# A third seven-product unit in the last two tiles of a fused attention and feed-forward kernel, and a prologue in another form

## The chip, the cores and the metric

The kernel runs on one core of one Trainium2 chip. The metric is the device time of one execution in microseconds, the median of three runs. In the profile, PE is TensorE (matmuls), PEld its weight loads, DVE is VectorE, ACT is ScalarE, POOL is GpSimd and SP is SyncE; L543 is line 543 of the kernel.

## The reference, cut to what matters

Attention over keys and values that are averaged in groups of eight rows, followed by a feed-forward layer with a silu:

```python
# q, k, v: 8 batches, 8 heads, 576 rows, 64 columns
k_p = k.reshape(B, H, Sp, pool, D).mean(axis=3)      # pool = 8, Sp = 72
v_p = v.reshape(B, H, Sp, pool, D).mean(axis=3)
scores = scale * np.matmul(q, k_p.transpose(0, 1, 3, 2))
attn = softmax(scores)
x = np.matmul(attn, v_p)                              # as 4608 tokens x 512
h = x @ w_in                                          # 512 x 2048
g = h * (1.0 / (1.0 + np.exp(-h)))
out = g @ w_out                                       # 2048 x 512, float32
```

## The kernel before: the parts that matter

The 4608 tokens are worked in nine tiles of 512 (t = 0 to 8), each with two stages. **up** computes h = x @ w_in and the silu, **down** computes g @ w_out. Work on the attention for the next tiles is put between the matmuls of both stages, as "fillers": a filler with number n is emitted ahead of step n + 1 of its stage. Each engine works its instructions in the order in which the program emits them.

```python
def spread(fillers, n):
    todo = sorted(fillers, key=lambda f: f[0])
    for i in range(n):
        yield i
        while todo and todo[0][0] <= i:
            todo.pop(0)[1]()
    for f in todo:
        f[1]()
```

The 2048 hidden columns are 16 groups of 128. A **plain** group takes four matmuls of 512 tokens (four steps) and a silu from PSUM. A **unit** takes four groups (two pairs) and 512 tokens as a 2 x 2 block product with seven products in place of eight (Strassen's scheme, in Winograd's way of sharing sums). A product is four matmuls of 256 columns (two steps). Sums of weight blocks are made once, sums of x blocks once for each tile, and VectorE and ScalarE combine the products:

```python
UNITS = ((4, 6), (8, 10))      # first groups of the two pairs of each unit
...
def stage(y, n):               # y: the unit; P, Q, R: PSUM banks of the unit
    if n == "2":
        product(y, 2, "P", True)
        nc.scalar.copy(r_sb, ps["P"])
    elif n == "5":
        product(y, 5, "Q", True)
        tt(out=rr_sb, in0=ps["Q"], in1=r_sb, op=ALU.add)
    elif n == "1":
        product(y, 1, "R", True)
        tt(out=t_sb, in0=ps["R"], in1=rr_sb, op=ALU.subtract)
    elif n == "4":
        product(y, 4, "P", False)
        hidden(y, 1, 0, ps["P"])              # silu, from PSUM
    elif n == "3":
        product(y, 3, "Q", False)
        hidden(y, 0, 1, ps["Q"])
    elif n == "7":
        product(y, 7, "P", False)
        tt(out=c_sb[0], in0=ps["P"], in1=t_sb, op=ALU.add)
    elif n == "6":
        product(y, 6, "Q", False)
        tt(out=c_sb[1], in0=ps["Q"], in1=t_sb, op=ALU.add)
    elif n == "h":
        hidden(y, 0, 0, c_sb[0])              # silu, from SBUF
    else:
        hidden(y, 1, 1, c_sb[1])
```

r_sb, rr_sb, t_sb and the two c_sb are single buffers that all units share. The order of an up stage from tile 2 on, where G(n) is a plain group and (y, "251") are products of unit y with their combining:

```python
items = (
    G(12, 13) + [(0, "251")] + G(14) + [(0, "43")] + G(15) + [(0, "76")]
    + [(1, "2")] + [(0, "hs")] + [(1, "51")] + G(0) + [(1, "43")] + G(1)
    + [(1, "7h6")] + G(2) + [(1, "s")] + G(3)
)
for n in U_X:                                  # five sums of x blocks
    f_up.append((0, lambda n=n: unit_x_sum(t, n)))
for n in (2, 5):
    f_up.append((36 if t > 1 else 45, lambda n=n: hidden_sum(n, 4, 8)))
f_up.append((56, lambda: hidden_sum(6, 4, 8)))
for n, k0 in ((2, 0), (5, 0), (1, 4), (1, 0)):
    f_up.append((64, lambda n=n, k0=k0: hidden_sum(n, k0, k0 + 4)))
```

down uses the same scheme over the whole tile: 7 products of 16 matmuls (112 steps), on five sums of hidden states (`h_sum`) which VectorE makes at the end of up and during down. It begins with products 2 and 5 in halves, so that the sums of the groups that are finished first are used first:

```python
product(2, KA, KQ)             # the sum of groups 4-7 and 12-15, later tokens
product(5, KA, KQ)
product(2, 0, KA)              # the sum of groups 0-3 and 8-11, later tokens
nc.scalar.copy(r_sb, ps["P"])
product(5, 0, KA)
tt(out=rr_sb, in0=ps["Q"], in1=r_sb, op=add)
...                            # products 1, 4, 3, 7, each with a copy or an add
product(6, 0, KQ, cc)
tt(out=o_sb[1][:, cs, HI], in0=ps["Q"][:, cs], in1=t_sb[:, cs], op=add)
```

PSUM has eight banks: three with the tag "mm" (plain groups, the R of a unit, P, Q and R of down) and five with the tag "at" (attention, P and Q of a unit).

The prologue keeps TensorE busy with dummy matmuls while the first keys load. `warm_up(n)` issues n dummies that wait for nothing; `warm_behind` issues dummies in float32 that read a part of the loaded keys and so wait for it:

```python
warm_up(9)
warm_behind(row_tiles["k"][0][:, SA - 1, RE - 128 :], 8)
slot_sums("k", 0)
select_k(0, 0)
copy_k(0, 0, act_copy)
warm_up(4)
...
load_w_in(1536, d_ff)
load_q(1)
...
def plain(t, step, g, n0, n):
    tag = "at" if (t, g, n0) == (0, 3, 0) else "mm"
    hp_ps = ps_tile([128, 512], FP32, tag, "hp_ps")
```

In tile 0 the groups are worked in pieces of 288 and 224 tokens, and the first silu comes after a load of ScalarE's table. The choice of tag in `plain` gives the fourth piece of tile 0 a bank of the other tag.

Of the kernel before, what the change touches and what calls it, by code (L numbers as in the profile page):

```python
# [36 lines left out]
def kernel(  # L37
# [53 lines left out]
    def ps_tile(shape, dtype, tag, name):  # L91
        return psum.tile(shape, dtype, tag=tag, bufs=banks[tag], name=name)
# [4 lines left out]
    ident = shifts[:, SP : SP + 128]  # L97
    ones = singles.tile([SP, 32], BF16, name="ones")
    warm = singles.tile([128, 512], BF16, name="warm")
    warm32 = singles.tile([128, 128], FP32, name="warm32")  # L100
    w_in_sb = singles.tile([128, KF, d_ff], BF16, name="w_in_sb")
    w_out_sb = singles.tile([128, KG, d_model], BF16, name="w_out_sb")
    w_sum = singles.tile([128, 5, KQ, CQ], BF16, name="w_sum")
# [8 lines left out]
    t_sb = singles.tile([128, 2, CQ], FP32, name="t_sb")  # L112
    xT = singles.tile([128, KF, NX], BF16, name="xT")

    w_sum1 = [singles.tile([128, 5, 2, 256], BF16, name=f"w_sum1{n}") for n in range(2)]
# [209 lines left out]
    def third(n):  # L325
        return tuple((g, n * QV, (n + 1) * QV) for g in range(2))
# [93 lines left out]

    UNITS = ((4, 6), (8, 10))
    UW = [
        {
            (i, j): w_in_sb[:, 2 * j : 2 * j + 2, 128 * u : 128 * (u + 2)]
# [14 lines left out]
    def unit_weight_sum(y, n):  # L441
        a, b = U_W[n]
        nc.vector.tensor_tensor(
            out=w_sum1[y][:, U_WI[n]], in0=UW[y][a], in1=UW[y][b],
            op=ALU.subtract if n in (6, 7) else ALU.add,
        )

# [6 lines left out]

    def unit_weights(y, n):
        if n in U_WI:
            return w_sum1[y][:, U_WI[n]]
        return UW[y][0, 0] if n == 3 else UW[y][1, 1]

    def unit_x(t, n):  # L460
# [5 lines left out]
    def up(t, fillers, items):  # L466
        step = spread(
            fillers,
            sum(
                KF if len(it) == 3 else 2 * len(it[1].strip("hs")) for it in items  # L470
            ),
        )
        ps = {}

        def product(y, n, bank, first):
            if first:
                tag = "mm" if bank == "R" else "at"
                ps[bank] = ps_tile([128, 2, NQ], FP32, tag, f"u_ps{bank}")
            w, x = unit_weights(y, n), unit_x(t, n)
            for u in range(2):  # L480
                next(step)
                for kk in range(2):
                    nc.tensor.matmul(  # L483
                        ps[bank][:, u, :], lhsT=w[:, kk, 128 * u : 128 * (u + 1)],
                        rhs=x[:, kk, :], start=first and u == 0 and kk == 0,
                        stop=kk == 1, skip_group_check=True,
                    )

        def hidden(y, i, j, src):
            g = UNITS[y][i]  # L490
            nc.scalar.activation(  # L491
                h_T[:, g : g + 2, j * NQ : (j + 1) * NQ], src, func=AF.Silu
            )

        tt = nc.vector.tensor_tensor

        def stage(y, n):
            if n == "2":
                product(y, 2, "P", True)
                nc.scalar.copy(r_sb, ps["P"])  # L500
            elif n == "5":
                product(y, 5, "Q", True)
                tt(out=rr_sb, in0=ps["Q"], in1=r_sb, op=ALU.add)
            elif n == "1":
                product(y, 1, "R", True)
                tt(out=t_sb, in0=ps["R"], in1=rr_sb, op=ALU.subtract)
            elif n == "4":
                product(y, 4, "P", False)
                hidden(y, 1, 0, ps["P"])
            elif n == "3":  # L510
                product(y, 3, "Q", False)
                hidden(y, 0, 1, ps["Q"])
            elif n == "7":
                product(y, 7, "P", False)
                tt(out=c_sb[0], in0=ps["P"], in1=t_sb, op=ALU.add)  # L515
            elif n == "6":
                product(y, 6, "Q", False)
                tt(out=c_sb[1], in0=ps["Q"], in1=t_sb, op=ALU.add)
            elif n == "h":
                hidden(y, 0, 0, c_sb[0])  # L520
            else:
                hidden(y, 1, 1, c_sb[1])

        for it in items:
            if len(it) == 3:
                plain(t, step, *it)
            else:
                for n in it[1]:
                    stage(it[0], n)
        for _ in step:  # L530
            pass

    def plain(t, step, g, n0, n):
        tag = "at" if (t, g, n0) == (0, 3, 0) else "mm"
        hp_ps = ps_tile([128, 512], FP32, tag, "hp_ps")
        c0 = (t * NTT + n0) % NX

        for r0, r1 in ((0, min(n, NX - c0)), (min(n, NX - c0), n)):
            for kk in range(KF) if r1 > r0 else ():
                if r0 == 0:  # L540
                    next(step)
                x0 = (c0 + r0) % NX
                nc.tensor.matmul(  # L543
                    hp_ps[:, r0:r1],
                    lhsT=w_in_sb[:, kk, g * 128 : (g + 1) * 128],
                    rhs=xT[:, kk, x0 : x0 + r1 - r0],
                    start=(kk == 0), stop=(kk == KF - 1),
                )
        nc.scalar.activation(h_T[:, g, n0 : n0 + n], hp_ps[:, :n], func=AF.Silu)  # L549
# [148 lines left out]
    def warm_up(n):  # L698
        for _ in range(n):
            nc.tensor.matmul(warm_ps, lhsT=warm[:, :128], rhs=warm, start=True, stop=True)  # L700

    def warm_behind(rhs, n):
        for _ in range(n):
            nc.tensor.matmul(  # L704
                warm_ps[:, : rhs.shape[-1]], lhsT=warm32, rhs=rhs, start=True, stop=True
            )
# [10 lines left out]
    load_slots(nc.gpsimd, 0, "v", 4, 5)  # L717
    attn_tables()
    nc.vector.memset(warm, 0.0)
    nc.vector.memset(warm32, 0.0)  # L720
    nc.vector.memset(ones, float(POOL))
    nc.vector.memset(kp, 0.0)
    nc.gpsimd.memset(shifts, 0.0)
# [5 lines left out]
    def load_w_in(c0, c1):  # L729
        for g in range(2):  # L730
            nc.gpsimd.dma_start(
                out=w_in_sb[:, 2 * g : 2 * g + 2, c0:c1], in_=w_in_r[g][:, :, c0:c1]
            )
# [6 lines left out]
        load_w_in(512 * c, 512 * (c + 1))  # L740

    act_copy = nc.scalar.copy
    warm_up(9)
    warm_behind(row_tiles["k"][0][:, SA - 1, RE - 128 :], 8)
    slot_sums("k", 0)
    select_k(0, 0)
    copy_k(0, 0, act_copy)
# [29 lines left out]
    load_slots(nc.gpsimd, 1, "k", 0, 3)  # L777
    load_slots(nc.gpsimd, 1, "k", 3, 4)
    load_slots(nc.gpsimd, 1, "k", 4, 5)
    load_w_in(1536, d_ff)  # L780
    load_q(1)
    for c in range(3):
        load_w_out(c)
    load_slots(nc.gpsimd, 1, "v", 0, 3)
# [4 lines left out]
    def load_half_2(name, half):  # L789
        for i0, i1 in ((0, SA), (SA, SLOTS), (SLOTS, SLOTS + 1)):  # L790
            load_slots(nc.gpsimd, 2, name, i0, i1, half)

    visits = [third(n) for n in range(3)]
    for t in range(NT):
        a = t + 1
        f_up, f_down = [], []
        if t == 0:
            GA = 11
            items = [(g, 0, HS) for g in range(GA)]
            items += [(g, HS, NTT - HS) for g in range(GA)]  # L800
            items += [(g, 0, NTT) for g in range(GA, KG)]
            f_up += [(1, lambda: denominators(0, part(0, 1), on_dve=True))]
            f_up += [(5, lambda: denominators(0, part(1, 1), on_dve=True))]
            f_up += [(13, lambda: numerators(0, part(0, 1)))]
            f_up += [(17, lambda: numerators(0, part(1, 1)))]
        else:
            G = lambda *gs: [(g, 0, NTT) for g in gs]
            if t == 1:
                items = (
                    G(12, 13, 14, 15) + [(0, "251")] + G(8) + [(0, "43")] + G(9)  # L810
                    + [(0, "7h6")] + G(10) + [(0, "s")] + G(11, 0, 1, 2, 3)
                )
            else:
                items = (
                    G(12, 13) + [(0, "251")] + G(14) + [(0, "43")] + G(15) + [(0, "76")]
                    + [(1, "2")] + [(0, "hs")] + [(1, "51")] + G(0) + [(1, "43")] + G(1)
                    + [(1, "7h6")] + G(2) + [(1, "s")] + G(3)
                )
            for n in U_X:
                f_up.append((0, lambda n=n: unit_x_sum(t, n)))  # L820
            for n in (2, 5):
                f_up.append((36 if t > 1 else 45, lambda n=n: hidden_sum(n, 4, 8)))
            f_up.append((56, lambda: hidden_sum(6, 4, 8)))
            for n, k0 in ((2, 0), (5, 0), (1, 4), (1, 0)):
                f_up.append((64, lambda n=n, k0=k0: hidden_sum(n, k0, k0 + 4)))
            f_down.append((33, lambda: hidden_sum(7, 0, 8)))
            f_down.append((71, lambda: hidden_sum(6, 0, 4)))
# [9 lines left out]
        if a < B:  # L837
# [50 lines left out]
            for n, sg in enumerate(visits):  # L888
                if n < 2 or not 0 < t < B - 2:
                    f_down.append((nu_at[n], lambda sg=sg: numerators(a, sg)))  # L890
                if n == 0 and 1 < t < B - 1:
                    f_down.append((nu_at[n], lambda: numerators(a - 1, visits[2])))
        moe_tables()
        up(t, f_up, items)
        if t == 0:
# [31 lines left out]
```

## Time and profile before

| | |
|---|---|
| time, median of 3 runs | 284.87 us (284.66 to 285.56) |
| span of the profiled execution | 283.6 us |
| TensorE busy | 276.2 us |
| VectorE busy | 225.8 us |
| ScalarE busy | 183.8 us |
| granted TensorE clock | 1.00 |

The largest groups of instructions:

```profile
L543 PE MATMUL hp_ps<-xT,w_in_sb 128*128 128x512 bf16 (+3 forms) x397 | 80.0, 338 | 1.0 <-issue 0.2
L651 PEld LDWEIGHTS <-h_sum 128*128 128x128 bf16 x640 | 60.6, 98 | 11.9 <-issue 1.3
L549 ACT ACTIVATE h_T<-hp_ps 128x512 bf16<-128x512 f32 (+2 forms) x95 | 51.5, 547 | 24.9 <-PE hp_ps L543 23.8
L611 DVE TENSOR_TENSOR h_sum<-h_T 128x1024 bf16<-128x1024 bf16 (+1 forms) x72 | 50.9, 744 | 7.0 <-ACT h_T L549 7.0
```

A line reads: line, engine, operation, what is written and read, shape, how often; then the busy us and the mean ns of one; then the idle time of the engine just ahead of it and what ended most of that. The ends of matmuls are modelled and overlap the next one, so the mean of a matmul is longer than the distance from one start to the next.

A line of a timeline reads: start and length in us, engine, line, operation, what is written and read, and how many instructions are merged in it; in brackets the idle time ahead of it.

### The profile page before, as it was taken

Reading aid. Unit: us, or ns where it says so; the run is one execution under the profiler, and the core shown is the slowest. Engines: PE = TensorE matmul, PEld = TensorE weight load, DVE = VectorE, ACT = ScalarE, POOL = GpSimd, SP = SyncE. Lnnn points to the kernel's source line nnn. Section 1 sums busy time; section 2 is a strip of 40 time slices with the busy share of each in tenths; the row PEclk is TensorE's granted clock in tenths of the full one; section 3 lists DMA queues with packets and bytes.
Section 4 is the critical chain, followed back from the end, with each engine's and each line's share of the span. In section 5 each row is a group of like instructions: output and inputs, shape, how many; then the busy total and the mean of one; then the engine's idle time right before and its main releaser. Section 6 shows DMA issues by size and latency. Waiting matters only on the chain.

```text
span 283.6 us, 6902 instructions
## 1 busy us (share of the span) xinstructions
PE 276.2 (97%) x2779; PEld 196.5 (69%) x2799; DVE 225.8 (80%) x405; ACT 183.8 (65%) x359; POOL 60.7 (21%) x78
## 2 busy tenths in 40 slices
PE   8989999999999999999999999999999999999995
PEld 4448544466777677767888786688667767787684
DVE  4888846899978898879896988799888786836773
ACT  1677766568567876687668857885779467326700
POOL 8565216242140214021402130551000000000000
PEclk9999999999999999999999999999999999999999
DMA  7999998896749862995498549497830041005003
GB/s 214 276 261 231 216 311 159 221 171 118 148 65 199 159 145 46 190 195 112 74 181 195 92 89 191 111 149 107 139 96 0 2 104 46 2 18 132 1 20 131
DMA packets 31376, 37.70 MB, mean 133 GB/s; under 512 B 10352, under 2 KB 22256, under 8 KB 31344
## 3 DMA queue, kind: packets, MB, share of 16 engines
q0 software_dynamic: 23840, 26.77, 52.4%
q1 hardware_dynamic: 6928, 9.58, 12.2%
q10 hardware_dynamic: 576, 0.92, 0.9%
q8 instruction: 22, 0.36, 0.5%
q14 instruction: 10, 0.08, 0.1%
HBM read 36.70 MB, written 9.44 MB: 163 GB/s over the span
## 4 chain that ended last, share of the span: by engine, by line
PE 94%; DVE 3%; ACT 1%; issue 1%; DVEq 0%
PE hp_ps L543 26%; PE o_psP L651 15%; PE o_psQ L651 15%; PE u_psP L483 7%; PE u_psQ L483 7%; PE o_psR L651 5%; PE sc_ps L346 4%; PE o_ps L578 3%; PE nu_ps L390 3%; PE warm_ps L700 2%; PE u_psR L483 2%; PE den_ps L364 2%; PE warm_ps L704 1%; DVE w_sum L629 1%; ACT es L354 1%
## 5 line engine op out<-in xcount | busy, mean ns | idle before, releaser
L543 PE MATMUL hp_ps<-xT,w_in_sb 128*128 128x512 bf16 (+3 forms) x397 | 80.0, 338 | 1.0 <-issue 0.2
L651 PEld LDWEIGHTS <-h_sum 128*128 128x128 bf16 x640 | 60.6, 98 | 11.9 <-issue 1.3
L549 ACT ACTIVATE h_T<-hp_ps 128x512 bf16<-128x512 f32 (+2 forms) x95 | 51.5, 547 | 24.9 <-PE hp_ps L543 23.8
L611 DVE TENSOR_TENSOR h_sum<-h_T 128x1024 bf16<-128x1024 bf16 (+1 forms) x72 | 50.9, 744 | 7.0 <-ACT h_T L549 7.0
L543 PEld LDWEIGHTS <-w_in_sb 128*128 128x128 bf16 x412 | 39.4, 98 | 24.3 <-issue 0.6
L354 ACT ACTIVATE es<-sc_ps 72x384 bf16<-72x384 f32 (+1 forms) x100 | 39.1, 470 | 10.0 <-PE sc_ps L346 9.9
L483 PEld LDWEIGHTS <-w_sum 128*128 128x128 bf16 x300 | 29.4, 98 | 7.6
L651 PEld LDWEIGHTS <-h_T 128*128 128x128 bf16 x256 | 24.1, 98 | 4.4 <-issue 0.9
L399 DVE TENSOR_TENSOR xT<-nu_ps,rec 128x384 bf16<-128x384 f32 (+1 forms) x50 | 23.9, 532 | 0.2
L373 ACT ACTIVATE lnd<-den_ps 128x384 f32<-128x384 f32 (+1 forms) x23 | 11.2, 485 | 19.3 <-PE den_ps L364 19.3
L154 DVE STREAM_TRANSPOSE qT<-q_bf 128x576 bf16<-128x576 bf16 x32 | 23.0, 755 | 0.2 <-DMA q_bf<-in_q_dram 0.2
L491 ACT ACTIVATE h_T<-c_sb 128x512 bf16<-128x512 f32 x30 | 18.1, 627 | 5.7 <-DVE c_sb L515 5.7
L269 DVE TENSOR_TENSOR raw<-raw 128x384 f32<-128x384 f32 (+3 forms) x20 | 12.4, 620 | 7.7 <-DMA raw<-in_v_dram 5.0
L178 POOL DMA_DIRECT2D raw<-in_k_dram x5 | 7.1, 1429 | 53.0 <-DMA raw<-in_k_dram 53.0
L651 PE MATMUL o_psP<-w_out_sb,h_sum 128*128 128x256 bf16 x128 | 17.6, 273 | 0.0
L555 POOL DMA_DIRECT2D out_dram<-o_sb x1 | 0.6, 617 | 79.4 <-issue 79.4
L515 DVE TENSOR_TENSOR c_sb<-u_psP,t_sb 128x512 f32<-128x512 f32 x15 | 10.3, 689 | 8.2 <-PE u_psP L483 3.6
L651 PE MATMUL o_psQ<-w_sum,h_sum 128*128 128x256 bf16 x128 | 16.7, 273 | 0.0
L651 PE MATMUL o_psQ<-w_out_sb,h_sum 128*128 128x256 bf16 x128 | 16.6, 273 | 0.0
L651 PE MATMUL o_psQ<-w_sum,h_T 128*128 128x256 bf16 x128 | 16.5, 273 | 0.0
L651 PE MATMUL o_psP<-w_sum,h_T 128*128 128x256 bf16 x128 | 16.5, 273 | 0.0
L651 PE MATMUL o_psR<-w_sum,h_sum 128*128 128x256 bf16 x128 | 15.7, 273 | 0.0
(83 smaller groups left out, 441.8 us busy)
## 6 DMA issues: line engine op xcount, KB each, us to landing
out_dram<-o_sb SPq DMA_DIRECT2D x128, 64.0 KB, 4.2
raw<-in_k_dram POOLq DMA_DIRECT2D x10, 576.0 KB, 9.9
raw<-in_v_dram POOLq DMA_DIRECT2D x10, 576.0 KB, 8.3
q_bf<-in_q_dram POOLq DMA_DIRECT2D x6, 576.0 KB, 13.5
w_in_sb<-in_moe_w_in_dram POOLq DMA_DIRECT2D x8, 256.0 KB, 8.3
w_out_sb<-in_moe_w_out_dram POOLq DMA_DIRECT2D x4, 512.0 KB, 13.5
raw<-in_v_dram POOLq DMA_DIRECT2D x2, 768.0 KB, 11.6
raw<-in_k_dram POOLq DMA_DIRECT2D x1, 768.0 KB, 9.8
```

Of the source, the lines that this page charges most:

```text
L154: nc.vector.transpose(out=st["qT"][:, a, f * QF : (f + 1) * QF].rearrange("r i c p -> r (i c p)"), in_=st["q_bf"][:, a, f * n : (f + 1) * n],)
L269: nc.vector.tensor_add(out=raw[..., :w], in0=raw[..., :w], in1=raw[..., w : 2 * w])
L346: nc.tensor.matmul(sc[s][:, cs], lhsT=kz[b % 2][rows, g, c, :], rhs=st["qT"][rows, g, i0:i1, c, :], start=(c == 0), stop=(c == 1),)
L354: nc.scalar.activation(es[:, s, :], sc[s], func=AF.Exp, scale=score_scale)
L373: nc.scalar.activation(lnd, den_ps[:, :w], func=AF.Ln)
L399: nc.vector.tensor_mul(out=xT[:, 2 * g0 + c : 2 * (g0 + ng - 1) + c + 1 : 2, cols], in0=nu[c][:, :w].rearrange("r (g n) -> r g n", g=ng), ...
L483: nc.tensor.matmul(ps[bank][:, u, :], lhsT=w[:, kk, 128 * u : 128 * (u + 1)], rhs=x[:, kk, :], start=first and u == 0 and kk == 0, stop=kk ...
L491: nc.scalar.activation(h_T[:, g : g + 2, j * NQ : (j + 1) * NQ], src, func=AF.Silu)
L543: nc.tensor.matmul(hp_ps[:, r0:r1], lhsT=w_in_sb[:, kk, g * 128 : (g + 1) * 128], rhs=xT[:, kk, x0 : x0 + r1 - r0], start=(kk == 0), stop= ...
L549: nc.scalar.activation(h_T[:, g, n0 : n0 + n], hp_ps[:, :n], func=AF.Silu)
L611: nc.vector.tensor_tensor(out=h_sum[n][:, ks, :], in0=quarter(*a, ks), in1=quarter(*b, ks), op=op)
L651: nc.tensor.matmul(ps[b][:, c, :], lhsT=left(n, kt, c), rhs=W_OUT[n][:, kt, :], start=b not in begun, stop=kt == k1 - 1, skip_group_check= ...
```

## The change

It takes groups 12 to 15 of the last two tiles (t = 7 and 8, where there is no attention work left for later tiles) as a third unit, so that only groups 0 to 3 stay plain. The products of the three units (A is the new one) are interleaved with one another, so that their combining on VectorE and ScalarE lies beside products of another unit. The sums of the new unit's weights go to buffers that the early tiles used for keys and values, and are made in down of tile 6, beside the copies of its outputs. The sums of x for tiles 7 and 8 are made in down of the tile ahead. The prologue takes another form: nineteen dummies that wait for nothing, q ahead of the last columns of w_in in the load queue, and all plain groups in "mm" banks. The purpose is less work for TensorE in the last two tiles.

```diff
-    warm32 = singles.tile([128, 128], FP32, name="warm32")
...
-    UNITS = ((4, 6), (8, 10))
+    UNITS = ((4, 6), (8, 10), (12, 14))
...
-                ps[bank] = ps_tile([128, 2, NQ], FP32, tag, f"u_ps{bank}")
+                ps[y, bank] = ps_tile([128, 2, NQ], FP32, tag, f"u_ps{bank}")
...
     def plain(t, step, g, n0, n):
-        tag = "at" if (t, g, n0) == (0, 3, 0) else "mm"
-        hp_ps = ps_tile([128, 512], FP32, tag, "hp_ps")
+        hp_ps = ps_tile([128, 512], FP32, "mm", "hp_ps")
...
-    warm_up(9)
-    warm_behind(row_tiles["k"][0][:, SA - 1, RE - 128 :], 8)
+    warm_up(19)
...
+    load_q(1)
     load_w_in(1536, d_ff)
-    load_q(1)
...
+    THREE = (
+        "g0 A2 A5 g1 A4 B2 A3 A1 B5 A7 C2 A6 B4 B3 B1 C5 Ah B7 As C4 Bh B6 C1 C3 C7 Bs"
+        " g2 C6 Ch Cs g3",
+        "A2 A5 g0 A4 B2 A3 A1 B5 A7 C2 A6 B4 B3 B1 C5 Ah B7 As C4 Bh B6 C1 C3 C7 Bs g1"
+        " C6 Ch Cs g2 g3",
+    )
...
+            elif t >= B - 1:
+                items = []
+                for it in THREE[t - B + 1].split():
+                    items += [(("BCA".index(it[0])), it[1])] if it[0] in "ABC" else G(int(it[1]))
...
-            for n in U_X:
-                f_up.append((0, lambda n=n: unit_x_sum(t, n)))
+            if t < B - 1:
+                for n in U_X:
+                    f_up.append((0, lambda n=n: unit_x_sum(t, n)))
             for n in (2, 5):
-                f_up.append((36 if t > 1 else 45, lambda n=n: hidden_sum(n, 4, 8)))
+                h_at = 50 if t >= B - 1 else 36 if t > 1 else 45
+                f_up.append((h_at, lambda n=n: hidden_sum(n, 4, 8)))
...
+        if t in (B - 2, B - 1):
+            for n in (4, 1, 3, 7, 6):
+                f_down.append((103 if t < B - 1 else 44, lambda n=n: unit_x_sum(t + 1, n)))
+        if t == B - 2:
+            k_w = big.tile([128, 4, 2, 256], BF16, tag="k_raw2", name="w_sum12")
+            v_w = big.tile([128, 4, 2, 256], BF16, tag="v_raw2", name="w_sum12")
+            w_sum1.append([k_w[:, i] for i in range(4)] + [v_w[:, 0]])
+            for i, n in enumerate(U_W):
+                f_down.append((73 if i < 2 else 81, lambda n=n: unit_weight_sum(2, n)))
```

B is 8, so t >= B - 1 means tiles 7 and 8, and t == B - 2 tile 6. The hidden states that the new unit gives are groups 12 to 15, which together with groups 4 to 7 make the sums that down reads first.

More of the change, by code (lines that the diff above doesn't have):

```diff
@@ L113 @@
     xT = singles.tile([128, KF, NX], BF16, name="xT")
-    w_sum1 = [singles.tile([128, 5, 2, 256], BF16, name=f"w_sum1{n}") for n in range(2)]
+    w_sum1 = [
+        [w[:, i] for i in range(5)] for w in (
+            singles.tile([128, 5, 2, 256], BF16, name=f"w_sum1{n}") for n in range(2)
+        )
+    ]
     x_sum = singles.tile([128, 5, 2, NQ], BF16, name="x_sum")
@@ L443, in unit_weight_sum @@
         nc.vector.tensor_tensor(
-            out=w_sum1[y][:, U_WI[n]], in0=UW[y][a], in1=UW[y][b],
+            out=w_sum1[y][U_WI[n]], in0=UW[y][a], in1=UW[y][b],
             op=ALU.subtract if n in (6, 7) else ALU.add,
@@ L456, in unit_weights @@
         if n in U_WI:
-            return w_sum1[y][:, U_WI[n]]
+            return w_sum1[y][U_WI[n]]
         return UW[y][0, 0] if n == 3 else UW[y][1, 1]
@@ L483, in product @@
                     nc.tensor.matmul(
-                        ps[bank][:, u, :], lhsT=w[:, kk, 128 * u : 128 * (u + 1)],
+                        ps[y, bank][:, u, :], lhsT=w[:, kk, 128 * u : 128 * (u + 1)],
                         rhs=x[:, kk, :], start=first and u == 0 and kk == 0,
@@ L499, in stage @@
                 product(y, 2, "P", True)
-                nc.scalar.copy(r_sb, ps["P"])
+                nc.scalar.copy(r_sb, ps[y, "P"])
             elif n == "5":
                 product(y, 5, "Q", True)
-                tt(out=rr_sb, in0=ps["Q"], in1=r_sb, op=ALU.add)
+                tt(out=rr_sb, in0=ps[y, "Q"], in1=r_sb, op=ALU.add)
             elif n == "1":
                 product(y, 1, "R", True)
-                tt(out=t_sb, in0=ps["R"], in1=rr_sb, op=ALU.subtract)
+                tt(out=t_sb, in0=ps[y, "R"], in1=rr_sb, op=ALU.subtract)
             elif n == "4":
                 product(y, 4, "P", False)
-                hidden(y, 1, 0, ps["P"])
+                hidden(y, 1, 0, ps[y, "P"])
             elif n == "3":
                 product(y, 3, "Q", False)
-                hidden(y, 0, 1, ps["Q"])
+                hidden(y, 0, 1, ps[y, "Q"])
             elif n == "7":
                 product(y, 7, "P", False)
-                tt(out=c_sb[0], in0=ps["P"], in1=t_sb, op=ALU.add)
+                tt(out=c_sb[0], in0=ps[y, "P"], in1=t_sb, op=ALU.add)
             elif n == "6":
                 product(y, 6, "Q", False)
-                tt(out=c_sb[1], in0=ps["Q"], in1=t_sb, op=ALU.add)
+                tt(out=c_sb[1], in0=ps[y, "Q"], in1=t_sb, op=ALU.add)
             elif n == "h":
@@ L700, in warm_up @@
             nc.tensor.matmul(warm_ps, lhsT=warm[:, :128], rhs=warm, start=True, stop=True)
[L702 to L706, printed above, removed]
     load_slots(nc.sync, 0, "k", 0, 2)
@@ L719 @@
     nc.vector.memset(warm, 0.0)
-    nc.vector.memset(warm32, 0.0)
     nc.vector.memset(ones, float(POOL))
@@ L791, in load_half_2 @@
             load_slots(nc.gpsimd, 2, name, i0, i1, half)
+    THREE = (
[3 more added lines that the diff above has]
+        " C6 Ch Cs g2 g3",
+    )
     visits = [third(n) for n in range(3)]
```

## The prediction

> **What bounds the kernel now.** I read the page first (busy shares, then the chain that ended last), then the stretches of the last two tiles, then the timelines of TensorE, VectorE and ScalarE there and in the first 22 us.
>
> ```profile
> span 283.6 us, 6902 instructions
> ...
> PE 276.2 (97%) x2779; PEld 196.5 (69%) x2799; DVE 225.8 (80%) x405; ACT 183.8 (65%) x359; POOL 60.7 (21%) x78
> ...
> PE 94%; DVE 3%; ACT 1%; issue 1%; DVEq 0%
> ...
> 229.13:242.15 13.02, 12.91 (x88) 8.61 (x88) 9.51 (x17) 8.97 (x18) 0.00 (x0) 1.00 0.26 67
> 242.15:254.42 12.27, 12.27 (x113) 10.82 (x112) 6.90 (x10) 3.40 (x5) 0.00 (x0) 1.00 0.01 1
> 254.42:267.44 13.02, 12.91 (x88) 8.60 (x88) 9.51 (x17) 8.84 (x17) 0.00 (x0) 1.00 0.32 82
> 267.44:279.86 12.42, 12.42 (x113) 10.71 (x111) 8.47 (x16) 1.53 (x3) 0.62 (x1) 1.00 0.14 50
> ```
>
> The chain is 94% TensorE: what TensorE neither does nor waits for is saved in full, and a wait of TensorE is lost in full. The four stretches are up and down of tiles 7 and 8 (edges from the TensorE timeline; columns: length, then busy us of PE, weight loads, DVE, ACT, POOL). An up of 13.02 us has no hole: 8 plain groups at 0.866 us (4 matmuls of 512 columns) are 6.93 and 2 units at 3.06 us (28 matmuls of 256 columns at 0.1094 us; sixteen take 1.75 us in the chain) are 6.13, in all 13.06. VectorE has 3.5 us free there, ScalarE 4.
>
> The seam between up and down of tile 7, VectorE (first group), ScalarE (second), TensorE (last three lines):
>
> ```profile
> 240.24 0.69 DVE L515 TENSOR_TENSOR c_sb<-u_psP,t_sb 128x512 f32<-128x512 f32 x1 [0.61 <-ACT h_T L491]
> 240.85 0.68 DVE L518 TENSOR_TENSOR c_sb<-u_psQ,t_sb 128x512 f32<-128x512 f32 x1
> ...
> 243.12 2.50 DVE L611 TENSOR_TENSOR h_sum<-h_T 128x1024 bf16<-128x1024 bf16 x4 [0.99 <-ACT h_T L549]
> ...
> 241.99 0.62 ACT L491 ACTIVATE h_T<-c_sb 128x512 bf16<-128x512 f32 x1
> 242.50 0.59 ACT L549 ACTIVATE h_T<-hp_ps 128x512 bf16<-128x512 f32 x1
> ...
> 240.42 1.89 PE L543 MATMUL hp_ps<-xT,w_in_sb 128*128 128x512 bf16 x8
> 242.15 1.04 PE L651 MATMUL o_psP<-w_out_sb,h_sum 128*128 128x256 bf16 x8
> ...
> 243.90 1.04 PE L651 MATMUL o_psP<-w_out_sb,h_sum 128*128 128x256 bf16 x8
> ```
>
> After product 6 of the last unit two plain groups follow (1.73 us); beside them VectorE adds c_sb, ScalarE makes the last silus (done 243.09), and VectorE makes the sum of tokens that the third run of down matmuls reads at 243.90. That sum is ready at 243.12 + 0.69 = 243.81: a margin of 0.1 us. This seam decides the case.
>
> And the prologue:
>
> ```profile
> 1.20 4.02 PE L700 MATMUL warm_ps<-warm 128*128 128x512 bf16 x9 [1.20 <-DVE warm L719]
> ...
> 5.01 3.02 PE L704 MATMUL warm_ps<-raw,warm 128*128 128x128 f32 x16
> ...
> 6.82 0.36 DVE L273 TENSOR_TENSOR k<-raw 128x192 bf16<-128x192 f32 x1
> ...
> 7.97 0.28 PE L291 MATMUL kz_ps<-shifts,k 128*32 128x72 bf16 x12
> ...
> 18.59 1.28 ACT L409 ACT_TABLE_LOAD   x1
> ...
> 19.02 1.16 PE L543 MATMUL hp_ps<-xT,w_in_sb 128*128 128x288 bf16 x8
> ...
> 19.88 1.46 ACT L549 ACTIVATE h_T<-hp_ps 128x288 bf16<-128x288 f32 x4
> ```
>
> k is ready at 7.18, but its selection waits until 7.97 behind dummies. The first silu of tile 0 can start only after a table load, at 19.88, while TensorE is already at its fourth piece at 19.76 (sixteen matmuls of 0.123 us; the fourth piece is the last two of the eight at 19.02, and two more).
>
> **What the Trainium skill says.** "TensorE: Matmul & The Clock Gate", section "Wait — 56ns, not 53.3ns?": start to start is columns over 2.4 GHz plus some 2.5 ns, so 109 and 216 ns for 256 and 512 columns; the trace agrees (109.4, 216.5). Its section "What's actually happening" says that the window after which a cold clock is released is free-running; here the dummies' loads went from 0.213 to 0.107 us apart at about 7.05 us. "VectorE: DVE Perf Modes", section "The perf-mode tier table", gives a bf16 tensor_tensor twice the rate of one with a PSUM operand: here 419 and 689 ns at 512 elements. "PSUM — Partial Sum Buffer", section "PSUM bank collisions raise a hardware error", asks for a wait by bank: a piece that takes a bank waits for its reader. The trace before avoids that at tile 0's fourth piece.
>
> **The change part by part.**
>
> 1. *Products.* In each of tiles 7 and 8 four plain groups (16 x 0.2165 = 3.46 us) become a unit (28 x 0.1094 = 3.06). Gain 0.40 us a tile, 0.80 in all.
>
> 2. *Weight sums of the unit, tile 6.* Five VectorE instructions at 0.34 us a start, two ahead of the third product's copy (VectorE idle 0.93 us there) and three behind it (idle 1.11). They fit: 0.
>
> 3. *Sums of x, a tile ahead.* Five at 0.34 in down of tile 6, ahead of the last output add, which moves from 229.33 to about 230.8. It holds one of the three "mm" banks. Tile 4 tells which group takes that bank: there the second plain group started at 141.90, the add ended at 141.92, and no hole shows, so it takes another; the third user comes at start + 3.9 us. In down of tile 7 they lie in an idle of 2.19 us. Cost 0; gain 0, as the plain groups hid them.
>
> 4. *VectorE and ScalarE in up.* Per up, VectorE loses 1.76 us of x sums and gets 4 adds (about 2.45), ScalarE gets one copy. I walked the order of tile 7 with plain 0.866, product 0.4375, 0.20/0.25 us from the end of a plain/product to its reader, 0.605 from add to add, some 0.5 from silu to silu. Until product 6 of the last unit no TensorE wait comes out.
>
> 5. *The seam of tile 7.* Only one plain group follows that product. From the up's start: 20 products and 2 plain groups put the end of the last unit's product 7 at 10.48, plain g2 at 11.34, product 6 at 11.78, g3 (the end, E) at 12.64. The two sums of hidden states set to step 50 fall inside g2 (steps 48 to 51), so ahead of the add after product 6 in VectorE's order. The first needs the second unit's last silu: that unit's product 6 ends at 9.16, its add runs 9.50 to 10.19, a silu from 10.29 goes ahead, so 10.79 to 11.42. The sums run 11.46 to 12.75, and the add, ready to go at 12.03, runs 12.67 to 13.36. Its silu ends at 14.02, the silu of g3, behind it, at 14.49, the sum of tokens starts at 14.53 and is ready at 15.21 + 0.05. TensorE wants it at E + 1.75 = 14.39. Wait: 0.87 us, and 0.07 more at the sixth product's sums. Loss 0.94.
>
> 6. *The seam of tile 8.* Two plain groups follow product 6, and step 50 lies behind its add. The same walk gives the add at 11.17, silus to 13.50, sum ready at 14.28 against 14.40 wanted: no wait.
>
> 7. *Fourth piece of tile 0 back in a "mm" bank.* It must wait for the silu of the first piece: 19.88 + 0.41 + 0.05 = 20.34 instead of 19.76. Loss 0.58, with nothing later to absorb it: VectorE at 46.3 us waits for TensorE itself.
>
> 8. *Dummies.* Nineteen, waiting for nothing: cold (0.427 each) until 7.05, then 0.216, gives 13.7 + 5.3 dummies and an end at 8.2, 0.2 later than 7.97. The sums of v, which a transfer releases at 13.53, absorb most: the add behind them starts at 14.92, and its other input was there by 14.6. Loss 0.05.
>
> 9. *Load of q ahead of the last columns of w_in.* q landed at 29.55, last of the two; now the weights land there, wanted from 30.7. 0.
>
> Sum: -0.80 + 0.94 + 0.58 + 0.05 = +0.77 us; 284.87 + 0.77 = 285.6.
>
> **Rivals.** (a) The seam of tile 7 holds, as the order was chosen with care: the gain of 0.80 stands against 0.63 in the prologue, 284.7. Against it: the margin before was 0.1 us, and here 0.87 us less lies behind product 6. (b) The last output add of tile 6 does hold the bank that tile 7's second group takes: g1 would wait until 231.5 instead of 230.87, 0.65 more, 286.3. The tile 4 coincidence speaks against it, by only some 0.07 us. (c) The prologue is bound by transfers (the DMA rows show full engines to 45 us) and steps 7 and 8 vanish: 285.0. Against it: from 21.6 to 46 us TensorE has no hole as long as 0.3 us. (d) The sums at step 50 find the silu in time and both seams hold, and the prologue is hidden too: 284.1.
>
> **Range and chances.** The sum has parts of half a microsecond with opposite signs; each may fail alone. The three times before spread over 0.9 us, which the phase of the clock's release in the prologue could explain. 284.4 to 286.5 holds all rivals but (d). No part comes near 2% (5.7 us): faster 0.01, same 0.98, slower 0.01.
>
> **What would show it.** Tile 7's up of about 12.65 us and tile 8's the same; a hole of some 0.9 us in TensorE 1.75 us after up of tile 7 ends, with VectorE's sum of hidden states as releaser, and none in tile 8; a hole of 0.6 us ahead of the fourth piece of tile 0, released by a silu. I am wrong if up and down of tile 7 together are under 25.0 us (25.29 before), or if the stretch to the first down matmul of tile 0 isn't later by about 0.6 us.

## The result, and the profile after

| | before | after |
|---|---|---|
| time, median of 6 runs each | 284.9 us (284.49 to 285.56) | 285.8 us (285.38 to 286.07) |
| ratio, 95% interval | | 1.0030 (1.0015 to 1.0044) |
| span of the profiled execution | 283.6 us | 284.2 us |

The changed kernel is slower by 0.3%, clear of noise. The page of the changed kernel and, below it, its up and down of tiles 7 and 8 as stretches (length, then busy us of PE, weight loads, DVE, ACT, POOL):

```profile
span 284.2 us, 6955 instructions
...
PE 275.7 (97%) x2797; PEld 196.8 (69%) x2817; DVE 232.1 (82%) x417; ACT 184.5 (65%) x361; POOL 60.6 (21%) x78
...
229.20:241.82 12.62, 12.52 (x100) 9.72 (x100) 10.09 (x19) 9.29 (x18) 0.00 (x0) 1.00 0.27 68
241.82:255.42 13.60, 12.46 (x114) 10.80 (x114) 10.30 (x18) 3.59 (x6) 0.00 (x0) 1.00 0.01 1
255.42:268.04 12.62, 12.52 (x100) 9.77 (x100) 9.38 (x15) 9.43 (x18) 0.00 (x0) 1.00 0.34 85
268.04:280.46 12.42, 12.41 (x113) 10.75 (x111) 9.41 (x18) 1.46 (x3) 0.61 (x1) 1.00 0.14 50
```

Both ups are 0.40 us shorter, 12.62 against 13.02: the third unit saves what its matmuls say. Down of tile 8 is unchanged at 12.42. Down of tile 7 is 13.60 against 12.27, 1.33 longer with the same 112 matmuls, so the difference is a hole. The timelines at that seam show it, VectorE first, then ScalarE, then TensorE:

```profile
238.83 0.68 DVE L521 TENSOR_TENSOR c_sb<-u_psQ,t_sb 128x512 f32<-128x512 f32 x1
239.62 0.69 DVE L509 TENSOR_TENSOR t_sb<-u_psR,rr_sb 128x512 f32<-128x512 f32 x1
240.44 0.69 DVE L518 TENSOR_TENSOR c_sb<-u_psP,t_sb 128x512 f32<-128x512 f32 x1
241.05 1.28 DVE L613 TENSOR_TENSOR h_sum<-h_T 128x1024 bf16<-128x1024 bf16 x2
242.25 0.69 DVE L521 TENSOR_TENSOR c_sb<-u_psQ,t_sb 128x512 f32<-128x512 f32 x1
242.85 0.68 DVE L613 TENSOR_TENSOR h_sum<-h_T 128x1024 bf16<-128x1024 bf16 x1
244.12 2.50 DVE L613 TENSOR_TENSOR h_sum<-h_T 128x1024 bf16<-128x1024 bf16 x4 [0.58 <-ACT h_T L551]
...
242.97 0.63 ACT L494 ACTIVATE h_T<-c_sb 128x512 bf16<-128x512 f32 x1 [1.13 <-DVE c_sb L521]
243.51 0.58 ACT L551 ACTIVATE h_T<-hp_ps 128x512 bf16<-128x512 f32 x1
...
240.96 1.03 PE L545 MATMUL hp_ps<-xT,w_in_sb 128*128 128x512 bf16 x4
241.82 1.04 PE L653 MATMUL o_psP<-w_out_sb,h_sum 128*128 128x256 bf16 x8
...
244.87 1.05 PE L653 MATMUL o_psP<-w_out_sb,h_sum 128*128 128x256 bf16 x8 [1.14 <-DVE h_sum L613]
```

Read it from the last line back. The second run of product 2 starts at 244.87; with no wait it would have been 241.82 + 16 x 0.1094 = 243.57, so TensorE waits 1.30 us between starts, for the sum that VectorE begins at 244.12. That waits for the silu of the last plain group (243.51), which is behind the silu from c_sb (242.97), which waits for the add at 242.25. The add's product ended at 240.96, and in front of it in VectorE's order are the two sums of 241.05.

The prologue of the changed kernel, TensorE from the third piece of tile 0 to the second run of numerators:

```profile
18.76 0.91 PE L545 MATMUL hp_ps<-xT,w_in_sb 128*128 128x288 bf16 x6
20.07 0.41 PE L545 MATMUL hp_ps<-xT,w_in_sb 128*128 128x288 bf16 x2 [0.40 <-ACT h_T L551]
...
21.36 0.43 PE L393 MATMUL nu_ps<-es,vp 72*32 72x288 bf16 x8
```

The second numerators in the kernel before:

```profile
21.07 0.63 PE L390 MATMUL nu_ps<-es,vp 72*32 72x288 bf16 x8
```

The fourth piece waits for the first silu: 20.07 where 18.76 + 6 x 0.1225 = 19.50 was due, 0.57 us late. But from the first hidden matmul (the first matmul of a plain group in tile 0) to what follows the second numerators it takes 4.37 us (17.35 to 21.72) against 4.02 before (17.61 to 21.63). Some 0.2 us come back, because the second run of numerators takes 0.43 us here and took 0.63 before.

In the two profiled executions, then: first hidden matmul 0.26 earlier and 0.35 more up to the end of the second numerators, and tile 7's up starts 0.07 later (229.20 against 229.13), tile 7 in all +0.93, tile 8 -0.40; together +0.60, the difference of the spans. The medians differ by 0.9. The first hidden matmul starts between 16.86 and 17.62 us in the fourteen profiles of this study, which blurs the times (what sets this start is found with the last experiment). Without it the comparison is sharper: from the first hidden matmul to the end of the span the kernel before takes 265.95 us and the changed one 266.81, 0.86 us more (by the stretches above, 280.46 - 17.35 against 279.86 - 17.61). This length, called the **rest of the span** below, is read beside the times.

### The profile page after: what moved, and what is told of

The parts are those of the page before. It is cut to its first block, busy times and chain, and to the rows that moved or that the text cites. A ratio compares the mean times of both kernels' runs of the same rounds, so it can differ in the third digit from the quotient of the medians.

```text
span 284.2 us, 6955 instructions
## 1 busy us (share of the span) xinstructions
PE 275.7 (97%) x2797; PEld 196.8 (69%) x2817; DVE 232.1 (82%) x417; ACT 184.5 (65%) x361; POOL 60.6 (21%) x78
## 4 chain that ended last, share of the span: by engine, by line
PE 86%; DVE 5%; DMA 3%; issue 2%; ACT 1%; POOL 1%; DVEq 0%; POOLq 0%
PE hp_ps L545 22%; PE o_psP L653 15%; PE o_psQ L653 15%; PE u_psP L486 7%; PE u_psQ L486 7%; PE o_psR L653 5%; PE sc_ps L349 4%; PE o_ps L580 3%; DMA raw<-in_v_dram 3%; PE u_psR L486 2%; PE nu_ps L393 2%; PE den_ps L367 2%; DVE xT L402 1%; DVE w_sum L631 1%; POOL q_bf L131 1%
## 5 line engine op out<-in xcount | busy, mean ns | idle before, releaser
L545 PE MATMUL hp_ps<-xT,w_in_sb 128*128 128x512 bf16 (+3 forms) x365 | 72.4, 335 | 1.3 <-ACT h_T L551 0.4
L551 ACT ACTIVATE h_T<-hp_ps 128x512 bf16<-128x512 f32 (+2 forms) x87 | 46.5, 541 | 19.3 <-PE hp_ps L545 17.3
L545 PEld LDWEIGHTS <-w_in_sb 128*128 128x128 bf16 x380 | 36.2, 98 | 22.2 <-issue 1.4
L486 PEld LDWEIGHTS <-w_sum 128*128 128x128 bf16 x340 | 33.3, 98 | 7.5
L494 ACT ACTIVATE h_T<-c_sb 128x512 bf16<-128x512 f32 x34 | 20.6, 627 | 6.2 <-DVE c_sb L518 5.0
L503 ACT COPY r_sb<-u_psP 128x512 f32<-128x512 f32 x17 | 9.9, 584 | 10.2 <-PE u_psP L486 7.6
L509 DVE TENSOR_TENSOR t_sb<-u_psR,rr_sb 128x512 f32<-128x512 f32 x17 | 11.8, 692 | 5.8 <-PE u_psR L486 4.1
```

The lines of the kernel that those rows point to most:

```text
L486: nc.tensor.matmul(ps[y, bank][:, u, :], lhsT=w[:, kk, 128 * u : 128 * (u + 1)], rhs=x[:, kk, :], start=first and u == 0 and kk == 0, stop ...
L494: nc.scalar.activation(h_T[:, g : g + 2, j * NQ : (j + 1) * NQ], src, func=AF.Silu)
L509: tt(out=t_sb, in0=ps[y, "R"], in1=rr_sb, op=ALU.subtract)
L545: nc.tensor.matmul(hp_ps[:, r0:r1], lhsT=w_in_sb[:, kk, g * 128 : (g + 1) * 128], rhs=xT[:, kk, x0 : x0 + r1 - r0], start=(kk == 0), stop= ...
```

## The experiments

Each run is the changed kernel with the edit that is shown. Every batch had runs of the kernel before beside it (medians 284.81 to 284.96), and ratios are against those.

**The bank of the fourth piece.**

```diff
-        hp_ps = ps_tile([128, 512], FP32, "mm", "hp_ps")
+        tag = "at" if (t, g, n0) == (0, 3, 0) else "mm"
+        hp_ps = ps_tile([128, 512], FP32, tag, "hp_ps")
```

> The changed kernel with one thing undone: the fourth piece of tile 0 again takes a bank of the other tag. My theory: the wait of 0.40 us for the first silu ahead of that piece goes (0.58 us between starts), but as the piece then holds one of the attention's banks, the second run of numerators waits some 0.2 us as before the change, so from the first hidden matmul to the end of those numerators 4.0 us against 4.37, and the time falls by 0.35 us, from 285.8 to about 285.4. Rival (the prologue is bound by transfers): the stretch shortens, but the time stays at 285.8.

285.52 us, ratio 1.0022 (1.0015 to 1.0028). TensorE in the first tile:

```profile
18.27 1.15 PE L546 MATMUL hp_ps<-xT,w_in_sb 128*128 128x288 bf16 x8
19.35 0.43 PE L393 MATMUL nu_ps<-es,vp 72*32 72x288 bf16 x8
...
20.31 0.63 PE L393 MATMUL nu_ps<-es,vp 72*32 72x288 bf16 x8
```

The eight matmuls run without a hole, the second numerators take 0.63 again, and the stretch from the first hidden matmul (16.86) is 4.01 us, as before. In all profiles of the study with this bank that line has 0.63, in all without it 0.43. So the bank is worth 0.36 us in this stretch. The rest of the span is 266.49 us, 0.32 less than in the changed kernel, so the gain reaches the end and the rival (transfers bind the prologue, the time stays) falls. The median fell by 0.3 us too, though the intervals overlap.

**The dummies.** `warm_up(9)` and `warm_behind(..., 8)` in place of `warm_up(19)`.

> The changed kernel with the dummies of before: nine that wait for nothing and eight that wait for the loaded keys. My theory: under 0.1 us either way, as the loads of v set the start of the first hidden matmul. Rival: the nineteen dummies hold the selection of k, and the dummies of before are worth 0.2 to 0.3 us, 285.5.

285.68 us, ratio 1.0028 (1.0017 to 1.0038): nothing that can be told from the changed kernel. k is selected at 7.75 us here and at 7.68 in the changed kernel.

**Buffers of their own for the units' intermediate sums.**

```diff
+    rr_of, t_of = [rr_sb] * 3, [t_sb] * 3
...
-                tt(out=rr_sb, in0=ps[y, "Q"], in1=r_sb, op=ALU.add)
+                tt(out=rr_of[y], in0=ps[y, "Q"], in1=r_sb, op=ALU.add)
...                                   # and so for t_sb
+        if t == B - 1:
+            own = big.tile([128, 4, 2, CQ], FP32, tag="k_raw", name="own")
+            rr_of[1:], t_of[1:] = [own[:, 0], own[:, 1]], [own[:, 2], own[:, 3]]
```

> The changed kernel with buffers of its own for each unit's two intermediate sums in tiles 7 and 8. In the changed kernel an add that writes what the add ahead of it reads starts 0.79 to 0.82 us behind it, where the others start 0.605 behind, and the seam of tile 7 waits 1.30 us where I had 0.87. My theory: the shared buffers are that difference; the distances of 0.82 where only a buffer is shared fall to 0.61, the wait at the seam falls to about 0.9 us and the time by 0.4, to 285.4. Rival (the distance is the engine's own for a change of operands): distances, wait and time stay.

285.41 us, ratio 1.0022 (1.0014 to 1.0030). VectorE ahead of the seam, and TensorE behind it:

```profile
238.91 0.69 DVE L522 TENSOR_TENSOR c_sb<-u_psQ,t_sb 128x512 f32<-128x512 f32 x1
239.52 0.68 DVE L510 TENSOR_TENSOR own<-u_psR,own 128x512 f32<-128x512 f32 x1
240.34 0.69 DVE L519 TENSOR_TENSOR c_sb<-u_psP,own 128x512 f32<-128x512 f32 x1
...
242.11 1.04 PE L654 MATMUL o_psP<-w_out_sb,h_sum 128*128 128x256 bf16 x8
...
244.76 1.05 PE L654 MATMUL o_psP<-w_out_sb,h_sum 128*128 128x256 bf16 x8 [0.73 <-DVE h_sum L614]
```

The add into t starts 0.61 behind the add ahead of it (238.91 to 239.52), where it was 0.79; the next one, which reads its result, stays 0.82 behind (240.34). The wait at the seam is 244.76 - 242.11 - 1.75 = 0.90 us in place of 1.30. The rival falls: the distance is the price of a dependence, and part of it was only a shared buffer. The time fell by 0.4 us with overlapping intervals; the rest of the span, 266.44 us, is 0.37 shorter.

**Two plain groups behind the last product in tile 7 too.** Tile 8's string of `THREE` in both places.

> The changed kernel with tile 8's order of the units in tile 7 too, so that two plain groups follow the last product and the two sums at step 50 lie behind its add. My theory (one plain group is too little, and the sums go ahead of the add): the wait of 1.30 us at the seam of tile 7 goes; at the start of tile 7, which now begins with a unit, VectorE still has the sums of x and the last output add in front of the first add, which costs TensorE up to 0.3 us; the time falls by 1.0 us, to 284.8. Rival (VectorE has too much work in tile 7, whatever the order): a wait of 0.5 us or more stays at the seam and the time falls by less than 0.6.

284.75 us, ratio 0.9997 (0.9989 to 1.0006): 1.05 us less than the changed kernel. VectorE at the start of tile 7, then TensorE there and at its seam:

```profile
228.59 1.76 DVE L453 TENSOR_TENSOR x_sum<-xT 128x512 bf16<-128x512 bf16 x5
230.26 0.69 DVE L688 TENSOR_TENSOR o_sb<-o_psQ,t_sb 128x512 f32<-128x512 f32 x1
230.87 0.68 DVE L506 TENSOR_TENSOR rr_sb<-u_psQ,r_sb 128x512 f32<-128x512 f32 x1
...
230.90 0.60 PE L486 MATMUL u_psP<-xT,w_sum 128*128 128x256 bf16 x4
231.60 0.60 PE L486 MATMUL u_psQ<-x_sum,w_in_sb 128*128 128x256 bf16 x4
...
241.61 1.04 PE L653 MATMUL o_psP<-w_out_sb,h_sum 128*128 128x256 bf16 x8
242.48 1.04 PE L653 MATMUL o_psQ<-w_out_sb,h_sum 128*128 128x256 bf16 x8
243.36 1.04 PE L653 MATMUL o_psP<-w_out_sb,h_sum 128*128 128x256 bf16 x8
```

At the seam each run follows the last after 0.87 us: no wait. At the start one product is 0.26 us late (231.60 where 231.34 was due), because VectorE had the sums of x and the last output add ahead of the first unit's add, which reads the bank Q that this product writes and ends at 231.55. The work of VectorE and ScalarE in tile 7 is the same as in the changed kernel, so it isn't too much; it was in the wrong place, and the rival falls. The rest of the span is 265.75 us, 1.06 less.

**Tile 7 without the third unit.** `t >= B` in place of `t >= B - 1` for the order, the sums of x and step 50, and no sums of x ahead of tile 7.

> The changed kernel with tile 7 as before (two units, eight plain groups, its sums of x at its own start); tile 8 keeps three units. My theory: the third unit is worth 0.40 us of TensorE in each tile, and in tile 7 the waits at the seam (1.30 + 0.05 us) outweigh it; so tile 7 gets 0.95 us shorter, and the time falls from 285.75 to about 284.8. Rival (the third unit doesn't pay in either tile): the time falls by 0.5 or less.

284.96 us, ratio 1.0005 (0.9997 to 1.0013): 0.84 less. Tile 7 takes 25.29 us as in the kernel before, up of tile 8 12.62. The unit pays in tile 8, and the prologue takes that back: the rest of the span is 265.90 us, 0.05 under the kernel before, which is -0.40 in tile 8 and the 0.35 of the bank. The rival falls.

**The two sums behind the last product's add.** Step 54 in place of 50 in tile 7.

> The changed kernel with the two sums of step 50 moved to step 54 in tile 7, behind the last product's add; one plain group still follows. My theory: both things make the wait, the single plain group and the sums ahead of the add. Then the wait at the second run of product 2 (1.30 us) nearly goes, and one of about 0.75 us comes ahead of the first run, as its sum now starts only at the end of the up; in all some 0.5 us less, 285.25. Rival A (the place of the two sums is all): no wait of over 0.2 us stays, and the time falls by 1.2. Rival B (one plain group alone is all): the waits stay at 1.3 in all.

285.39 us, ratio 1.0016 (1.0009 to 1.0023): 0.4 less. TensorE at the seam:

```profile
241.21 1.03 PE L545 MATMUL hp_ps<-xT,w_in_sb 128*128 128x512 bf16 x4
242.83 1.05 PE L653 MATMUL o_psP<-w_out_sb,h_sum 128*128 128x256 bf16 x8 [0.59 <-DVE h_sum L613]
243.71 1.04 PE L653 MATMUL o_psQ<-w_out_sb,h_sum 128*128 128x256 bf16 x8
244.64 1.05 PE L653 MATMUL o_psP<-w_out_sb,h_sum 128*128 128x256 bf16 x8
```

The first run of product 2 now waits: 242.83 where 241.21 + 0.87 = 242.08 was due, 0.75 us. The second waits 0.06, so 0.81 in all in place of 1.30, and both rivals fall. Both causes are real: with one plain group behind the last product either the add or the sums came late, and of the orders tried only those with two plain groups there remove both.

**Both tiles in tile 8's order, the sums moved.** The sums of x for tile 7 need what is ready from step 56 of down of tile 6 on, so they can take the place of the weight sums; those can be made at any time.

```diff
-                f_down.append((103 if t < B - 1 else 44, lambda n=n: unit_x_sum(t + 1, n)))
+                x_at = 44 if t == B - 1 else 73 if n in (4, 1) else 81
+                f_down.append((x_at, lambda n=n: unit_x_sum(t + 1, n)))
...
+                for n, w_at in ((2, 44), (5, 44)) if t == B - 3 else ((1, 44), (6, 44), (7, 58)):
+                    f_up.append((w_at, lambda n=n: unit_weight_sum(2, n)))
```

> Tile 8's order in tile 7 too (as in the run with two plain groups last), and the sums of x for tile 7 at steps 73 and 81 of down of tile 6, where the weight sums were; the weight sums go to up of tiles 5 and 6, into idle stretches of VectorE of 0.96 and 0.99 us. My theory: the 0.26 us that TensorE waited at the start of tile 7 in that run goes too, and the time is 284.5. Rival (VectorE has no room in tiles 5 and 6): 0.3 us or more is lost there, at their seams, and the time is 284.75 or more.

284.15 us, ratio 0.9971 (0.9961 to 0.9982), lower than expected by 0.35. Against the run with two plain groups last the medians fall by 0.60, but the traces by 0.36 (rest of the span 265.39 against 265.75): 0.26 at the start of tile 7 and 0.10 in down of tile 6 (16.49 us against 16.60; the run with the dummies of before has 16.49 too, without the sums moved, so it need not be their doing). The executions with a profile, 284.41 and 284.08, differ by 0.33. The thirteen times of the earlier run reach up to 285.27, these eight only to 284.61; the remainder lies in executions without a profile. In tile 7 TensorE has no wait: up begins at 228.65 and down at 241.28, 12.63 us. VectorE's weight sums lie in idle stretches; the one of tile 5:

```profile
179.26 1.28 DVE L613 TENSOR_TENSOR h_sum<-h_T 128x1024 bf16<-128x1024 bf16 x2
180.47 0.75 DVE L446 TENSOR_TENSOR w_sum<-w_in_sb 128x512 bf16<-128x512 bf16 x2
181.15 0.69 DVE L518 TENSOR_TENSOR c_sb<-u_psP,t_sb 128x512 f32<-128x512 f32 x1
```

They cost TensorE nothing: down of tile 6 begins 195.28 us behind the first hidden matmul, and 195.27 in the run with two plain groups last. The rival falls.

**The same, with the bank of before, and with the whole prologue of before.**

> The same, and the fourth piece of tile 0 in the bank of before. My theory: the gains add up, another 0.3 us, 284.2, which is below the kernel before by 0.7. Rival: the two gains share a cause and the time stays at 284.5.

> Tile 8's order in both tiles, the sums moved, and the whole prologue of before. My theory: the same as with the bank alone, 284.0 to 284.1, which is 0.8 us (two gains of 0.40 us) below the kernel before. Rival: another 0.2 us or more from the dummies and the order of loads.

284.04 us, ratio 0.9965 (0.9953 to 0.9977), and 283.82 us, ratio 0.9959 (0.9946 to 0.9973). Both are faster than both kernels. The step of 0.3 us that was expected from the bank is 0.1 here by the medians, with overlapping intervals. The traces, one profile each, say more: the first hidden matmul started 0.65 us later in the profile with the bank of before (17.53 against 16.88), and its rest of the span is 265.01 us against 265.39, 0.38 less. With the whole prologue of before it is 265.00, so dummies and load order add nothing to that.

**The changed kernel with the whole prologue of before.**

> The changed kernel with the whole prologue of before (bank of the fourth piece, dummies, order of the loads of q and w_in), so that against the kernel before only the last two tiles and the sums for them differ. My theory: of the prologue only the bank counts, so the time is that of the run with the bank alone, 285.5; against the kernel before that is -0.40 us in tile 8 and +0.95 in tile 7. Rival (the order of the loads or the dummies count too): 285.2 or less.

285.54 us, ratio 1.0024 (1.0016 to 1.0033), as with the bank alone; the rest of the span is 266.51 us, against 266.49. So dummies and load order of before don't show, and most of the loss comes from the last two tiles: 0.7 of 0.9 us by the medians, 0.56 of 0.86 (266.51 - 265.95) by the rest of the span. The seam's wait is there again: the second run of product 2 starts at 244.49, 3.04 us after the first instead of 1.75.

**Fourteen dummies.** With nineteen dummies the selection of k behind them and the first hidden matmul move together. The starts of the two in the eight profiles with nineteen, in us: 7.27/16.86, 7.29/16.88, 7.32/16.86, 7.68/17.35, 8.06/17.48, 8.11/17.53, 8.17/17.59, 8.20/17.62. So the dummies that end late may hold the real work after all. `warm_up(14)` in place of `warm_up(19)`, in the changed kernel, and in the version with the sums moved and the bank of before:

> The changed kernel with fourteen dummies ahead of the keys in place of nineteen. In the profiles so far with nineteen, k is ready at 7.2 us and is selected between 7.27 and 8.20, and the first hidden matmul follows 9.4 to 9.7 us behind the selection (16.86 to 17.62). My theory, which corrects step 8 of the prediction: the dummies, at the cold clock for a part that differs from run to run, set the selection, and it sets the first hidden matmul. Fourteen end by 1.20 + 14 x 0.427 = 7.18 even if all are cold; so k is selected at 7.25 at the latest, the first hidden matmul starts at 16.9 in each run, and the time falls by some 0.3 us on average, to 285.5, with less spread. Rival (the landing of v sets it, and selection and start move together for another reason): the start is still anywhere in 16.9 to 17.6. Rival (five dummies fewer leave the clock cold for longer): later than 17.6.

> Tile 8's order in both tiles, the sums moved, the bank of before for the fourth piece, and fourteen dummies. My theory: as for the fourteen above, 0.2 to 0.3 us below the same kernel with nineteen (284.04), 283.8. Rival: no difference, 284.0.

285.63 us, ratio 1.0025 (1.0016 to 1.0035), and 283.69 us, ratio 0.9963 (0.9949 to 0.9976). These medians are 0.2 and 0.35 us below those with nineteen, within the intervals. TensorE at its start with nineteen, in the run with the intermediate sums' own buffers, the last sums of v on VectorE, which wait for a load, and the first hidden matmul:

```profile
1.20 7.07 PE L703 MATMUL warm_ps<-warm 128*128 128x512 bf16 x19 [1.20 <-DVE warm L716]
8.20 0.28 PE L295 MATMUL kz_ps<-shifts,k 128*32 128x72 bf16 x12
...
12.86 1.15 DVE L273 TENSOR_TENSOR raw<-raw 128x512 f32<-128x512 f32 x2 [0.22 <-DMA raw<-in_v_dram]
...
17.62 0.41 PE L546 MATMUL hp_ps<-xT,w_in_sb 128*128 128x288 bf16 x2
```

And in the changed kernel with fourteen:

```profile
1.20 6.00 PE L702 MATMUL warm_ps<-warm 128*128 128x512 bf16 x14 [1.20 <-DVE warm L715]
7.28 0.28 PE L294 MATMUL kz_ps<-shifts,k 128*32 128x72 bf16 x12
...
12.83 1.15 DVE L272 TENSOR_TENSOR raw<-raw 128x512 f32<-128x512 f32 x2 [0.34 <-DMA raw<-in_v_dram]
...
16.92 0.41 PE L545 MATMUL hp_ps<-xT,w_in_sb 128*128 128x288 bf16 x2
```

Fourteen in 6.00 us are all at the low clock (0.427 us apart), and yet k is selected at 7.28. The sums of v start at the same time in both runs, and the first hidden matmul 0.70 us earlier with fourteen. So a late release of the clock can reach the start of the real work by way of the dummies.

But this is one of two waits. In each of the fourteen profiles the first hidden matmul starts, to 0.01 us, at the later of two moments: 9.42 us behind the selection of k, or 4.09 us behind the start of the last sums of v. The selection comes last in six profiles: the dummies of before, own buffers, tile 7 without the third unit, the sums behind the last add, and, with the sums moved, the bank of before and the whole prologue of before. The sums of v come last in the other eight, among them the two kernels that are compared, with sums at 13.53 before and 13.26 after (17.61 and 17.35 for the first hidden matmul), and both runs with fourteen. So the rival that v sets the start is right for these, and the expected 16.9 in each run did not come: in the other run with fourteen k is selected at 7.29, the sums of v start at 13.00 and the first hidden matmul at 17.09. In the changed kernel with the whole prologue of before k was selected as early as 7.25, and the start was still 17.28, with the sums of v at 13.19. Fewer dummies can take away only one of the two delays, and whether the median gains by it the intervals don't settle.

## Why the prediction was right, and where its terms were off

It said 285.6 us, 0.77 slower, and that two holes decide: 285.8 was measured, 0.9 slower, with those holes where it put them.

1. *Products* (0.40 us a tile): 0.40 in both, from the lengths of the ups.
2. *Weight sums* at no cost: held; the output adds around them start as before.
3. *Sums of x* at no cost: held. The output add of tile 6 moved to 230.74 as said, and the second plain group started at 230.94, ahead of that add's end at 231.43, so it takes another bank, and rival (b) falls.
4. *The walk of VectorE in up*: here a size was off. It took 0.605 us from every add to the next. An add that reads or overwrites what the add ahead of it touches starts 0.79 to 0.82 behind. The last unit's first c_sb add therefore came at 240.44, or 11.24 us into the up, not at 10.73 (the end of its product at 10.48 and 0.25). The two sums behind it started at 11.85 (241.05) where the walk had 11.46, although the silu that the walk had them wait for ended in time.
5. *The seam of tile 7* (0.94 us): the cause was right, the size 1.30 + 0.05. With the shared buffers removed the wait is 0.90 us, against 0.87 in the prediction; so the missing 0.4 us is the term of step 4, as a run showed.
6. *The seam of tile 8* at no cost: held; both runs are 0.87 us apart.
7. *The fourth piece* (0.58 us): the wait was 0.57. What the step missed is that the other bank had a price of its own, 0.2 us at the second numerators; net 0.32 to 0.38 in the rest of the span. So the sign of being wrong that the prediction gave for the prologue did show: the first down matmul of tile 0 came at 34.09 us against 34.01 before, only 0.08 later and not 0.6, with 0.26 us less up to the first hidden matmul and 0.34 more behind it. That the numerators wait for a bank was not tested by itself; only that the 0.2 us come and go with it.
8. *Dummies* (0.05): for the two profiled executions the reasoning held. The sums of v set the first hidden matmul in both, and its start 0.26 us earlier is their earlier start (13.26 against 13.53), no doing of the dummies. What the step missed is that it is not so in every execution: the selection of k lies anywhere between 7.27 and 8.20 with nineteen dummies, and between 7.25 and 7.97 with those of before, and where it comes late it sets the start, as in six of the fourteen profiles.
9. *Load order* at no cost: held; with the sums moved, the rest of the span is 265.00 us with the whole prologue of before and 265.01 with its bank alone.

So the seam was taken 0.4 us too small and the prologue 0.3 too large. That the sum came out so near is in part luck: two errors of opposite sign nearly cancel. Rival (a), that the seam holds, falls; it held only with two plain groups behind the last product. Rival (c), that steps 7 and 8 vanish, falls too: 0.32 to 0.38 us of step 7 reach the end of the span. Rival (d) falls with (a).

## What to carry to other kernels

When a product is taken out of a bound engine, look at the seam where its last result is combined: what counts is how much work of the bound engine lies behind the last product, and what other engines have queued ahead of the combining. Instructions that can run later should go behind the one that is waited for, and if then something else is late, more independent work has to be moved behind the last product. An engine that is 80% busy in a stage can still be late at its end.

## What the runs showed of the hardware

VectorE starts an add of 512 float32 0.605 us behind an independent one, and 0.79 to 0.82 us behind one whose output it reads or whose input it overwrites. A buffer that two such chains share costs the 0.2 us even when no value passes. The start of the first hidden matmul differs by up to 0.76 us between profiles (16.86 to 17.62 us). Two things move it: the moment at which the clock is released (the starts of dummies go from 0.427 to 0.216 us apart, and nineteen took from 5.6 to 7.1 us) and the start of the last sums of v, which mostly wait for a load (12.64 to 13.53 us). Differences of under half a microsecond need the lengths of stretches in the trace beside the times: here the rest of the span behind that start agrees within 0.02 us between versions that differ in dummies and load order alone (266.81 and 266.83; 266.49 and 266.51; 265.00, 265.01 and 265.02), with one exception of 0.17 (266.64, the dummies of before in the changed kernel), while the times of one version spread over 0.6 to 1.4 us.
